# AFNO inverse on quarters of the TensorE array, and a remainder that is reordered through scratch

## The chip, the cores and the metric

The kernel runs on one core of one Trainium2 chip. The metric is the device time of one execution in microseconds: 1413.34 us before the change (median of 3 runs, 1412.42 to 1414.71). The engines are named as in the profile: PE (TensorE matmul), PEld (its weight loads), DVE (VectorE), ACT (ScalarE), POOL (GpSimd) and SP (SyncE, which only issues transfers here).

## The reference

One block on x of 4096 tokens with 640 channels. A condition vector c gives six modulation rows. First a spectral layer (AFNO): layer norm, modulation, a real FFT over the 4096 tokens, a two-layer complex MLP on each frequency in 4 blocks of 160 channels, a soft shrink, the inverse FFT. Then a SwiGLU feed-forward layer.

```python
Xf = rfft2(x, axes=(1, 2));  z = Xf.reshape(B, H, Wf, NB, BS);  zr, zi = z.real, z.imag
hr = relu(zr @ w1[0] - zi @ w1[1] + b1[0]);  hi = relu(zi @ w1[0] + zr @ w1[1] + b1[1])
or_ = hr @ w2[0] - hi @ w2[1] + b2[0];       oi_ = hi @ w2[0] + hr @ w2[1] + b2[1]
or_, oi_ = softshrink(or_, 0.01), softshrink(oi_, 0.01)
A = irfft2(or_ + 1j * oi_, s=(H, W), axes=(1, 2))

h = layernorm(x) * (1 + ca) + sa;   x = x + ga * A(h)
h = layernorm(x) * (1 + cb) + sb;   x = x + gb * ((silu(h @ w_gate) * (h @ w_up)) @ w_down)
```

## The kernel before

**Two parts.** The spectral part fills the first 310 us or so of the profiled execution, the feed-forward part the rest. The change is in the spectral part alone.

**The spectral part.** The transform over 4096 = 128 x 32 tokens is done in two factors. The first (`dft_a`) writes its result to scratch in DRAM (`s1`). The frequencies are then worked through in 8 chunks of 4 blocks, 32 places `p` in all, with chunk `ch = p // 4` and block `b = p % 4`. Chunk 4 (`CE`) has two more columns, for the frequencies that the others don't hold.

For a chunk, `load_g` fetches its part of `s1` and `stage_b` applies the second factor: five products `pb` per chunk, `t` = 0 to 3 for the first 128 channels of each block, and `t` = 4 for the **remainder**, the last 32 channels of all four blocks together on 128 partitions. `stage_l1` is the first MLP layer of a block, `stage_l2` the second, whose sums go to `tt`.

**fp32 from split parts.** The two layers need fp32 accuracy from fast fp32r products. An operand is split into a high part (the value rounded to fp32r by an ACT copy) and a low part (the difference, by DVE), and high x high, low x high and high x low are summed. `evac_b` makes both parts `z` of one `pb`. The remainder is different: `stage_l1` wants, for each block, the high parts of its 32 real and 32 imaginary rows and the low parts of both, one below the other, as one operand `rz` of 128 rows. `evac_rh` (ACT, line 630) and `evac_rl` (DVE, line 640) copy it 32 rows at a time, two ACT and two DVE instructions per block.

**The inverse.** After the last block of a chunk, `move_x` moves `tt` into four tiles `xx` (by DMA within SBUF, 64 real rows above 64 imaginary rows), `shrink_parts` (ACT) and `shrink` (DVE) do the soft shrink, `shrink_high` (ACT, line 752) and `shrink_low` (DVE, line 757) split `xx` into `xh` and `xl`. `stage_i` then applies the inverse of the second factor with the constant matrix `bm`, itself in a high and a low part: three fp32r products of 128 rows by 128 columns on each half of the 640 channels (lines 768 to 770), two ACT copies into `co`, and a store of `co` to scratch `s2` by POOL's queue. The matrix has two independent blocks of 64 x 64, for the two values of the index `p` in `constants()`; the rest of it is zero. Chunk 7, the last, has its inverse done in another way (`inverse_last`, line 825: fp32 products on 64 rows with the matrix `bx`).

**What sets the order.** The order of this part is written out by hand, place by place, in one loop over `p`; each engine executes its own instructions in that order and waits by semaphores. In a place stand the L1 layer of block `p`, the `stage_b` of a later block, the L2 layer of block `p - 1` and the inverse of `p - 7`. All transfers named here, but the stores of `co`, are issued by SP, in program order: a DMA that waits holds up those behind it. The first places also see SP finish the stores of `s1` (line 355), which precede `idn`, `tx` and `bx`. `fst`, `first_mm` and the lines from 947 on prepare the feed-forward part; they need the last `s2` rows (`load_first_rows`, line 832).

Memory places: SBUF pools hold tiles by tag with a number of buffers; a tag that changes size would shift its neighbours.

Of the kernel before, what the change touches and what calls it, by code (L numbers as in the profile page):

```python
# [6 lines left out]
F32 = mybir.dt.float32  # L7
# [39 lines left out]
def constants():  # L47
# [65 lines left out]
    bm = bm.reshape(2, 128, 128)  # L113
    bi = bm[1].reshape(2, 64, 128)

    bx = np.tile(bm[1].reshape(2, 64, 128).transpose(1, 0, 2), (2, 1, 1)).reshape(128, 256)
# [57 lines left out]
def body(tc, x, w1, b1, w2, b2, wg, wu, wd, c, wm, k_fa, k_tb, k_tx, k_bm, k_bx, k_ga, k_ge, k_id, out, dbg=None):  # L174
# [27 lines left out]
    with ExitStack() as top:  # L202
# [35 lines left out]
        with ExitStack() as af:  # L238
# [4 lines left out]
            bm = wp.tile([P, 2, 2, 128], F32R, name="bm")  # L243
# [345 lines left out]
            hss = {}  # L589

# [12 lines left out]
            def evac_b(ch, t):  # L603
                pb = pbs[ch, t]
                z = lp.tile([P, 2, 2, 258], F32R, tag="z", bufs=4, name=f"z{ch}_{t}")
                zs[ch, t] = z
                act.activation(z[:, 0, :, 0:256], pb, AF.Identity, scale=ca1[:, t:t + 1])
                dve.scalar_tensor_tensor(z[:, 1, :, 0:256], pb, ca1[:, t:t + 1],
                                         f32(z[:, 0, :, 0:256]), op0=OP.mult, op1=OP.subtract)
# [12 lines left out]
            def evac_rh(ch, b):  # L622
                pb = pbs[ch, 4]
                if b == 0:
                    rzs[ch] = hp.tile([P, NB, 258], F32R, tag="rz", bufs=2, name=f"rz{ch}")
                    if ch == CE:
                        pool.tensor_copy(rzs[ch][:, :, 257], zero.rearrange("p a b c d -> p (a b c d)")[:, 0:4])
                q = slice(32 * b, 32 * b + 32)
                for i in range(2):
                    act.activation(rzs[ch][32 * i:32 * i + 32, b, 0:256], pb[q, i, :], AF.Identity,  # L630
                                   scale=ca1[q, 4:5])

            def evac_rl(ch, b):
                pb = pbs[ch, 4]
                r = rzs[ch]
                q = slice(32 * b, 32 * b + 32)
                for i in range(2):
                    rh = slice(32 * i, 32 * i + 32)
                    rl = slice(64 + 32 * i, 96 + 32 * i)
                    dve.scalar_tensor_tensor(r[rl, b, 0:256], pb[q, i, :], ca1[q, 4:5],  # L640
                                             f32(r[rh, b, 0:256]), op0=OP.mult, op1=OP.subtract)
                    if ch == CE:
                        pool.tensor_copy(r[rh, b, 0:257:256], f32(edge[q, 0, 4, i]))
                        pool.tensor_copy(r[rl, b, 0:257:256], f32(edge[q, 1, 4, i]))
# [82 lines left out]
            def move_x(ch, i):  # L727
                q, h = i // 2, i % 2
                xx = p2.tile([P, D], F32, tag="xx", bufs=5, name=f"xx{ch}_{i}")
                for r in range(2):  # L730
                    nc.sync.dma_start(xx[64 * r:64 * r + 64, :], tts[ch, q][64 * h:64 * h + 64, r, :])
                xxs[ch, i] = xx
# [15 lines left out]
            def shrink_high(ch, i):  # L748
                xx = xxs[ch, i]
                xh = p2.tile([P, D], F32R, tag="xh", bufs=2, name=f"xh{ch}_{i}")  # L750
                xl = p2.tile([P, D], F32R, tag="xl", bufs=2, name=f"xl{ch}_{i}")
                act.activation(xh, xx, AF.Copy)
                xxs[ch, i] = (xh, xl, xx)

            def shrink_low(ch, i):
                xh, xl, xx = xxs[ch, i]
                dve.tensor_tensor(xl, xx, f32(xh), op=OP.subtract)

            def stage_i(ch, i):
                J = 4 * ORDER[ch] + i  # L760
                kd = 0 if J == 0 else 1
                xh, xl, _ = xxs[ch, i]
                co = p2.tile([P, D], F32, tag="xh" if 4 * ch + i == LAST - 1 else "co", bufs=2, name=f"co{J}")
                for hf in range(2):
                    e = slice(320 * hf, 320 * hf + 320)
                    pi = (bank0(0, [P, 512], f"pi{J}_{hf}") if ch == NCH - 2 and i % 2 and hf == 0 else
                          ps.tile([P, 512], F32, tag="p3", name=f"pi{J}_{hf}"))
                    mm(pi[:, :320], bm[:, kd, 0, :], xh[:, e], start=True, stop=False)
                    mm(pi[:, :320], bm[:, kd, 0, :], xl[:, e], start=False, stop=False)
                    mm(pi[:, :320], bm[:, kd, 1, :], xh[:, e], start=False, stop=True)  # L770
                    act.activation(co[:, e], pi[:, :320], AF.Copy)  # L771
                pool.dma_start(s2[4 * J:4 * J + 4].rearrange("k n d -> (k n) d"), co)  # L772
# [64 lines left out]
            for p in range(LAST + 1):  # L837
# [19 lines left out]
                rows = [p + 2] * (p < 4) + [p + 3] * (p > 2)  # L857
# [4 lines left out]
                for f in (shrink_high, tail_l1) if p == LAST else (tail_l1, shrink_high):  # L862
                    on(f, p if f == tail_l1 else p - 6)
# [4 lines left out]
                if p == LAST:  # L868
                    on(shrink_low, p - 6)
# [11 lines left out]
                on(stage_i, p - 7)  # L881
                if p < LAST:
                    on(shrink_low, p - 6)
                    on(shrink_parts, p - 5)
                if b == 0 and ch:
                    for i in range(4):
                        move_x(ch - 1, i)
                if p == 0:
# [3 lines left out]
                    pool.dma_start(bm.rearrange("p a b c -> p (a b c)"), k_bm)  # L892
# [11 lines left out]

            def load_first():
# [5 lines left out]
            for f in (shrink, shrink_high, shrink_low):  # L911
                on(f, LAST - 5)
            on(stage_i, LAST - 6)
            for p in range(LAST + 1, NP):
# [3 lines left out]
                if p == NP - 1:  # L918
                    on(shrink_high, p - 5)
                on(tail_l1, p)  # L920
                if p == NP - 1:
                    on(shrink_low, p - 5)
# [14 lines left out]
                if p < NP - 1:  # L937
                    on(shrink_high, p - 5)
                on(stage_l2, p - 1)
                on(stage_i, p - 6)  # L940
                if p < NP - 1:
                    on(shrink_low, p - 5)
            on(shrink, LAST - 1)
            on(shrink_high, LAST - 1)
# [4 lines left out]
            on(shrink_low, LAST - 1)  # L949
# [62 lines left out]
            for i in range(3):  # L1012
                xns[0].append(p2.tile([P, D], F32, tag="co" if i < 2 else "wm", bufs=2 if i < 2 else 1, name=f"xn0_{i}"))
# [1525 lines left out]
```

## Time and profile before

| | us |
|---|---|
| timed runs | 1412.42, 1413.34, 1414.71 |
| profiled execution, first to last instruction (the page gives no other time for it) | 1409.5 |
| median of the timed runs less that span | 3.8 |
| PE busy in it | 1382.5 (98%) |
| the loop from 109 to 257 us: PE, ACT, DVE busy of 148.0 | 147.95, 140.88, 131.67 |
| the 56 halves of the inverse: ACT copies of the result (line 771) | 22.6 |
| clock of PE over the span | 1.00 |

Rows of a timeline give the start, the time from the first start to the last end, engine, line, operation, output<-inputs, shape and count; matmuls are pipelined, so that a row's length is longer than what it adds. Rows of groups give the busy time, the mean ns of one, and the idle time before them with what ended it. Rows of transfers give the count, the size of each and the median time from issue to landing. In product shapes, 64*128 is 64 rows of the array by 128 columns. `SPq` is SP's queue of issues.

### The profile page before, as it was taken

How to read it: one execution, taken by the hardware profiler on the slowest of the kernel's cores; microseconds unless marked ns; L12 is line 12 of the kernel's file. 1: busy time of each engine (PE TensorE's matmuls, PEld its weight loads, DVE VectorE, ACT ScalarE, POOL GpSimd, SP SyncE). 2: the span in 40 equal slices, each digit the busy share in tenths (PEclk: the TensorE clock that was granted, in tenths of full speed). 3: DMA queues.
4: the chain of work that ended last, by engine and by line, in shares of the span. 5: the costliest groups of instructions: out<-in, count | busy, mean ns of one | idle time of the engine just before them, and what ended most of it. 6: DMA issues, size and time to landing. Idle time of an engine off the chain costs nothing. (4 is left out here: it accounts for less than half of the span.)

```text
span 1409.5 us, 23754 instructions
## 1 busy us (share of the span) xinstructions
PE 1382.5 (98%) x8410; PEld 1310.7 (93%) x8410; DVE 1067.8 (76%) x1861; ACT 765.0 (54%) x1542; POOL 604.6 (43%) x683
## 2 busy tenths in 40 slices
PE   6899999999999999999999999999999999999998
PEld 2599999967999889899999999999999999999998
DVE  8889888889888888649787668678678757375644
ACT  6879999755555554436454345546164624262341
POOL 5700200157766594326445534447153624042241
PEclk9999999999999999999999999999999999999999
DMA  9876466675998897898877998696998668956634
GB/s 371 310 244 211 157 196 193 203 232 170 327 353 308 308 335 263 293 368 308 308 225 281 375 330 288 236 326 230 375 330 309 217 218 282 350 194 217 199 115 149
DMA packets 171016, 377.34 MB, mean 268 GB/s; under 512 B 22193, under 2 KB 81649, under 8 KB 168882
## 3 DMA queue, kind: packets, MB, share of 16 engines
q1 hardware_dynamic: 161794, 359.28, 73.6%
q0 software_dynamic: 6800, 13.93, 3.1%
q10 hardware_dynamic: 2304, 2.62, 0.5%
q8 instruction: 66, 1.08, 0.3%
q14 instruction: 52, 0.43, 0.1%
HBM read 269.48 MB, written 96.80 MB: 260 GB/s over the span
## 5 line engine op out<-in xcount | busy, mean ns | idle before, releaser
L1442 DVE TENSOR_TENSOR wb<-r,wb 128x768 fp32r<-128x768 f32 (+3 forms) x170 | 170.4, 1013 | 13.5 <-ACT wb L1435 13.3
L2050 PE MATMUL pw<-h,wt 128*128 128x384 f32 x412 | 139.3, 338 | 0.6 <-ACT s_y L2069 0.6
L2052 PE MATMUL pw<-h,wt 128*128 128x384 f32 x412 | 138.3, 336 | 0.0
L2051 PE MATMUL pw<-h,wt 128*128 128x384 f32 x412 | 138.1, 335 | 0.0
L1435 ACT ACTIVATE wb<-r 128x768 fp32r<-128x768 f32 (+3 forms) x168 | 104.5, 639 | 56.3 <-PE pw L2063 41.7
L2351 PE MATMUL pc<-wq,L 128*128 128x320 f32 x846 | 132.7, 309 | 0.9 <-DMA wq<-wqd 0.9
L2110 POOL TENSOR_TENSOR sg<-s_x,sg 128x384 f32<-128x384 f32 x24 | 30.0, 1250 | 234.5 <-DVE s_x L2076 234.5
L2351 PEld LDWEIGHTS pc<-wq,L 128*128 128x128 f32 x846 | 126.3, 188 | 1.1 <-DVE x L2308 1.1
L2130 DVE TENSOR_TENSOR L<-sg,L 128x384 fp32r<-128x384 f32 x144 | 101.0, 725 | 27.7 <-ACT L L2126 27.2
L2069 ACT ACTIVATE s_x<-pw 128x384 f32<-128x384 f32 x52 | 25.6, 492 | 164.2 <-PE pw L2052 162.3
L2050 PE MATMUL pw<-h,wb 128*128 128x384 f32 x312 | 105.0, 336 | 0.0
L2051 PE MATMUL pw<-h,wb 128*128 128x384 f32 x312 | 104.4, 335 | 0.0
L2052 PE MATMUL pw<-h,wb 128*128 128x384 f32 x312 | 104.4, 335 | 0.0
L2121 POOL TENSOR_TENSOR sg<-sg,sg 128x384 f32<-128x384 f32 x72 | 91.9, 1276 | 23.4 <-DVE L L2130 20.0
L1973 PE MATMUL pg<-ht,wb 128*128 128x512 f32 x260 | 101.8, 392 | 0.0
L2351 PE MATMUL pe<-wq,L 128*128 128x320 f32 x648 | 101.7, 309 | 0.0
L1974 PE MATMUL pg<-ht,wb 128*128 128x512 f32 x260 | 101.3, 390 | 0.0
L1975 PE MATMUL pg<-ht,wb 128*128 128x512 f32 x260 | 101.2, 389 | 0.0
L2267 PE MATMUL pd<-wq,a 128*128 128x320 f32 x632 | 96.8, 310 | 0.0
L2351 PEld LDWEIGHTS pe<-wq,L 128*128 128x128 f32 x648 | 96.6, 188 | 0.0
L2267 PEld LDWEIGHTS pd<-wq,a 128*128 128x128 f32 x632 | 93.5, 188 | 0.5
L772 POOL DMA_DIRECT2D s<-co x28 | 15.7, 559 | 175.9 <-ACT co L771 175.9
(317 smaller groups left out, 3914.1 us busy)
## 6 DMA issues: line engine op xcount, KB each, us to landing
wq<-wqd SPq DMA_DIRECT2D x83, 640.0 KB, 6.1
wt<-td SPq DMA_DIRECT2D x103, 512.0 KB, 5.4
hs<-ho SPq DMA_DIRECT2D x52, 512.0 KB, 5.2
h<-hs SPq DMA_DIRECT2D x32, 768.0 KB, 7.9
td<-wt SPq DMA_DIRECT2D x25, 512.0 KB, 6.3
r<-in_B_w_gate_dram SPq DMA_DIRECT2D x24, 384.0 KB, 4.4
r<-in_B_w_up_dram SPq DMA_DIRECT2D x24, 384.0 KB, 4.3
xx<-tt SPq DMA_DIRECT2D x56, 160.0 KB, 3.3
```

The source lines that it names most:

```text
L1435: def high(ks, e=slice(0, c), copy=lambda o, i: act.activation(o, i, AF.Copy)):
L1442: dve.tensor_tensor(wbs[t, n][:, 1, ks, e], raw[t, n][:, ks, e], f32(wbs[t, n][:, 0, ks, e]), op=OP.subtract)
L1973: mm(b, wh, hh, start=(kk == 0), stop=False)
L1974: mm(b, wh, hl, start=False, stop=False)
L1975: mm(b, wl, hh, start=False, stop=(kk == 4))
L2050: mm(b, w(0, kp), a[:, kp, 0], start=start and kp == 0, stop=False, skip_group_check=not start)
L2051: mm(b, w(0, kp), a[:, kp, 1], start=False, stop=False, skip_group_check=not start)
L2052: mm(b, w(1, kp), a[:, kp, 0], start=False, stop=kp == 1, skip_group_check=not start)
L2121: pool.tensor_tensor(o, x, y, op=op)
L2130: dve.tensor_tensor(o[:, 1], raws[j], f32(o[:, 0]), op=OP.subtract)
L2267: mm(b[:, :320], l, m, start=start and i == 0, stop=stop and i == len(s) - 1)
L2351: mm(o[:, :320], ls[q][:, x, k], w[:, q, y], start=start and q == 0 and n == 0, stop=q == 1 and n == 2, skip_group_check=not start)
```

## The change

**Inverse.** `bm` becomes one fp32 matrix without parts: for each of the two blocks (`u`) on its 64 rows, the two variants `kd` of 64 columns. `xx` keeps real and imaginary rows interleaved as they stand in `tt`, so one DMA of 64 x 2 rows replaces two. `shrink_high` and `shrink_low` are gone. `stage_i` makes four fp32 products of 64 rows by 64 columns: block `u` takes rows `64u`, channel half `e` goes to the output rows `64e`, so that each of the four uses another quarter of the array; the two `u` write two PSUM banks, `e` the two halves of their partitions. The store is two DMAs of 64 partitions, with runs of 320 elements in place of 640. `stage_i` comes one place earlier (`p - 6`).

**Remainder.** Chunk 0 keeps its copies of 32 rows. For chunks 1 to 7 the remainder is evacuated by one `evac_b` like the other four, into a tile `zr`, and `move_r` writes its four parts (high real, high imaginary, low real, low imaginary; 128 partitions x 1 KB each) to scratch `rzd` and reads them back as `rz` in the wanted order: four DMAs out, one in, all on SP at the end of the place in which it is evacuated.

**Places.** `bm` is loaded by SP in place of POOL. The freed tags are balanced by a third buffer for `co` and a tile `spare`, so that other tiles stay where they are.

PE in the loop, the end of one place and the inverse in it (here the first place of chunk 3; `pc` is the L2 layer, `pi` the inverse, `pl` the L1 layer of the next place). Before:

```order
L711 MATMUL pc_0_1_1521<-w2a,h_0_0_1352 128x320 x3
L711 MATMUL pc_0_1_1521<-w2b,h_0_1_1366 128x320 x3
L711 MATMUL pc_0_1_1521<-w2c,r_2_0_1378 128x320 x2
L768 MATMUL pi_0_1532<-xh_2_1392,bm 128x320
L769 MATMUL pi_0_1532<-xl_2_1393,bm 128x320
L770 MATMUL pi_0_1532<-xh_2_1392,bm 128x320
L768 MATMUL pi_1_1537<-xh_2_1392,bm 128x320
L769 MATMUL pi_1_1537<-xl_2_1393,bm 128x320
L770 MATMUL pi_1_1537<-xh_2_1392,bm 128x320
L661 MATMUL pl_2_0_1551<-z_2_1287,w1a 128x256 x3
```

The same place with the change:

```order
L717 MATMUL pc_0_1_1489<-w2a,h_0_0_1338 128x320 x3
L717 MATMUL pc_0_1_1489<-w2b,h_0_1_1352 128x320 x3
L717 MATMUL pc_0_1_1489<-w2c,r_2_0_1364 128x320 x2
L763 MATMUL pi_0_1500<-xx_3_1060,bm 64x320
L763 MATMUL pi_1_1501<-xx_3_1060,bm 64x320
L763 MATMUL pi_0_1500<-xx_3_1060,bm 64x320
L763 MATMUL pi_1_1501<-xx_3_1060,bm 64x320
L667 MATMUL pl_2_0_1523<-z_2_1282,w1a 128x256 x3
```

Six products became four, between the same neighbours, and the tile is that of the next block (`xx_3`, not the parts of `xx_2`).

SP from the last store of `s1` to the first moves of `xx` (places 0 to 4). Before:

```order
L355 DMA s<-xa_122 64x4x640
L508 DMA idn<-in_k_id_dram 128x128
L509 DMA tx<-in_k_tx_dram 128x2
L531 DMA bx<-in_k_bx_dram 128x256
L308 DMA g_898<-s 128x1x2560
L298 DMA tb_900<-in_k_tb_dram 128x512
L536 DMA wm_0_987<-in_w_mod_dram 128x640
L731 DMA xx_0_1062<-tt_0_797 64x640 x2
```

With the change:

```order
L353 DMA s<-xa_122 64x4x640
L506 DMA idn<-in_k_id_dram 128x128
L507 DMA tx<-in_k_tx_dram 128x2
L529 DMA bx<-in_k_bx_dram 128x256
L886 DMA bm<-in_k_bm_dram 128x128
L623 DMA rzd<-z_4_863 4x32x256 x4
L625 DMA rz_900<-rzd 128x4x256
L306 DMA g_902<-s 128x1x2560
L296 DMA tb_904<-in_k_tb_dram 128x512
L534 DMA wm_0_983<-in_w_mod_dram 128x640
L736 DMA xx_0_1054<-tt_0_797 128x1x640
```

`bm`, the four stores of chunk 1's remainder and the load behind them now stand between `bx` and the load of `g` for chunk 2.

```diff
-    bm = bm.reshape(2, 128, 128)
     bi = bm[1].reshape(2, 64, 128)
-    bmh, bml = _hl(bm)
-    bm = np.stack([bmh, bml], axis=1)
-    bm = np.ascontiguousarray(bm.transpose(2, 0, 1, 3)).reshape(128, 2 * 2 * 128)
+    bm = np.stack([bm[:, :, u, :, u].reshape(2, 64, 64) for u in range(2)])
+    bm = bm.reshape(2, 2, 2, 32, 64).transpose(0, 3, 2, 1, 4).reshape(128, 128)
...
+            rzd = [nc.dram_tensor(f"rzd{i}", (4, 32, NB, 258), F32, kind="Internal").ap() for i in range(2)]
...
-                z = lp.tile([P, 2, 2, 258], F32R, tag="z", bufs=4, name=f"z{ch}_{t}")
+                z = (lp.tile([P, 2, 2, 258], F32R, tag="z", bufs=4, name=f"z{ch}_{t}") if t < 4 else
+                     hp.tile([P, 2, 2, 258], F32R, tag="zr", bufs=1, name=f"z{ch}_{t}"))
...
+            def new_r(ch):
+                rzs[ch] = hp.tile([P, NB, 258], F32R, tag="rz", bufs=2, name=f"rz{ch}")
+
+            def move_r(ch):
+                NN = width(ch)
+                d = rzd[ch % 2]
+                for q in range(4):
+                    nc.sync.dma_start(d[q, :, :, :NN].rearrange("r b e -> b r e"), f32(zs[ch, 4][:, q // 2, q % 2, :NN]))
+                new_r(ch)
+                nc.sync.dma_start(f32(rzs[ch][:, :, :NN]), d[:, :, :, :NN].rearrange("q r b e -> (q r) b e"))
...
-                for r in range(2):
-                    nc.sync.dma_start(xx[64 * r:64 * r + 64, :], tts[ch, q][64 * h:64 * h + 64, r, :])
+                nc.sync.dma_start(xx, tts[ch, q][64 * h:64 * h + 64])
...
             def stage_i(ch, i):
                 J = 4 * ORDER[ch] + i
                 kd = 0 if J == 0 else 1
-                xh, xl, _ = xxs[ch, i]
-                co = p2.tile([P, D], F32, tag="xh" if 4 * ch + i == LAST - 1 else "co", bufs=2, name=f"co{J}")
-                for hf in range(2):
-                    e = slice(320 * hf, 320 * hf + 320)
-                    pi = (bank0(0, [P, 512], f"pi{J}_{hf}") if ch == NCH - 2 and i % 2 and hf == 0 else
-                          ps.tile([P, 512], F32, tag="p3", name=f"pi{J}_{hf}"))
-                    mm(pi[:, :320], bm[:, kd, 0, :], xh[:, e], start=True, stop=False)
-                    mm(pi[:, :320], bm[:, kd, 0, :], xl[:, e], start=False, stop=False)
-                    mm(pi[:, :320], bm[:, kd, 1, :], xh[:, e], start=False, stop=True)
-                    act.activation(co[:, e], pi[:, :320], AF.Copy)
-                pool.dma_start(s2[4 * J:4 * J + 4].rearrange("k n d -> (k n) d"), co)
+                xx = xxs[ch, i]
+                co = p2.tile([P, 2, 320], F32, tag="co", bufs=3, name=f"co{J}")
+                pi = [bank0(0, [P, 512], f"pi{J}_0") if ch == NCH - 2 and i % 2 and u == 0 else
+                      ps.tile([P, 512], F32, tag="p3", name=f"pi{J}_{u}") for u in range(2)]
+                for e in range(2):
+                    for u in range(2):
+                        k = slice(64 * u, 64 * u + 64)
+                        mm(pi[u][64 * e:64 * e + 64, :320], bm[k, kd], xx[k, 320 * e:320 * e + 320], start=True, stop=True)
+                for u in range(2):
+                    act.activation(co[:, u], pi[u][:, :320], AF.Copy)
+                for e in range(2):
+                    pool.dma_start(s2[4 * J:4 * J + 4, :, 320 * e:320 * e + 320].rearrange("(u k) n d -> (k n) u d", u=2),
+                                   co[64 * e:64 * e + 64])
...
                 for q in todo:
                     stage_b(*q)
-                    if q[1] < 4:
+                    if q[1] < 4 or q[0]:
                         evac_b(*q)
...
-                rows = [p + 2] * (p < 4) + [p + 3] * (p > 2)
+                rows = [p + 2] * (p < 2)
...
-                on(stage_i, p - 7)
+                on(stage_i, p - 6)
...
+                if todo and todo[0][1] == 4:
+                    move_r(todo[0][0])
...
-                    pool.dma_start(bm.rearrange("p a b c -> p (a b c)"), k_bm)
+                    nc.sync.dma_start(bm.rearrange("p a b -> p (a b)"), k_bm)
...
+            p2.tile([P, 3 * D], F32, name="spare")
```

`shrink_high` and `shrink_low` and all calls of them are removed.

More of the change, by code (lines that the diff above doesn't have):

```diff
@@ L242, in body @@
             w1c = qp.tile([P, NB, 640], F32R, tag="wq", name="w1c")
-            bm = wp.tile([P, 2, 2, 128], F32R, name="bm")
+            bm = wp.tile([P, 2, 2, 128], F32, name="bm")[:, 0, 0].rearrange("p (a b) -> p a b", a=2)
             tx = wp.tile([P, 2], F32, name="tx")
@@ L624, in evac_rh @@
                 if b == 0:
[L625 to L627 removed]
+                    new_r(ch)
                 q = slice(32 * b, 32 * b + 32)
@@ L746, in shrink @@
                     dve.tensor_tensor(xx, xx, cl, op=OP.subtract)
[L748 to L757, printed above, removed]
             def stage_i(ch, i):
@@ L861, in body @@
                     weights_high(*prep2[4])
-                for f in (shrink_high, tail_l1) if p == LAST else (tail_l1, shrink_high):
-                    on(f, p if f == tail_l1 else p - 6)
+                on(tail_l1, p)
                 if p == 0:
@@ L908, in load_first @@
                 x2s[0] = x2
-            for f in (shrink, shrink_high, shrink_low):
-                on(f, LAST - 5)
-            on(stage_i, LAST - 6)
+            on(shrink, LAST - 5)
             for p in range(LAST + 1, NP):
```

20 lines of the change are left out of this document (2 added, 18 removed).

## The prediction

> **What bounds the kernel now.** I read the table of stretches first, since a mean over the whole span mixes stages; then the order of events of one step; then groups, transfers and the last steps of the spectral part.
>
> ```profile
> PE 1382.5 (98%) x8410; PEld 1310.7 (93%) x8410; DVE 1067.8 (76%) x1861; ACT 765.0 (54%) x1542; POOL 604.6 (43%) x683
> 109.00:257.00 148.00, 147.95 (x1159) 147.06 (x1158) 131.67 (x253) 140.88 (x289) 17.51 (x52) 1.00 0.60 193
> ```
>
> The second row (length, then busy time of PE, weight loads, DVE, ACT, POOL, then clock and DMA share) covers most of the loop that the change edits. PE is busy for 147.95 of 148.00 us. ACT is close behind (140.88), DVE too (131.67), but neither makes PE wait: work taken off them is worth nothing there. What counts is the time of the inverse on PE, and any wait that is new.
>
> ```profile
> 152.42 0.31 PE L768 MATMUL pi<-xh,bm 128*128 128x320 f32 x1
> 152.57 0.31 PE L769 MATMUL pi<-xl,bm 128*128 128x320 f32 x1
> ...
> 153.16 0.31 PE L770 MATMUL pi<-xh,bm 128*128 128x320 f32 x1
> 153.30 0.52 PE L661 MATMUL pl<-z,w1a 128*128 128x256 f32 x3
> ...
> 159.04 0.30 PE L768 MATMUL pi<-xh,bm 128*128 128x320 f32 x1
> ```
>
> One inverse occupies PE from 152.42 to 153.30, 0.88 us, six products 0.15 apart. A whole step of the loop is 159.04 - 152.42 = 6.6 us.
>
> **The change part by part. 1: split parts and remainder copies go.**
>
> ```profile
> L752 ACT ACTIVATE xh<-xx 128x640 fp32r<-128x640 f32 x28 | 20.3, 726 | 6.7 <-DVE xx L746 6.5
> L757 DVE TENSOR_TENSOR xl<-xx,xh 128x640 fp32r<-128x640 f32 x28 | 22.8, 814 | 0.9 <-ACT xh L752 0.8
> L630 ACT ACTIVATE rz<-pb,ca 32x256 fp32r<-32x256 f32 x64 | 29.8, 466 | 1.6 <-DVE rz L640 0.5 <-PE pb L600 0.2
> L640 DVE SCALAR_TENSOR_TENSOR rz<-pb,ca,rz 32x256 fp32r<-32x256 f32 x64 | 30.9, 483 | 7.1 <-ACT rz L630 5.9
> L607 ACT ACTIVATE z<-pb,ca 128x512 fp32r<-128x512 f32 x32 | 22.1, 689 | 6.4 <-PE pb L600 5.7
> L608 DVE SCALAR_TENSOR_TENSOR z<-pb,ca,z 128x512 fp32r<-128x512 f32 x32 | 24.0, 749 | 10.2 <-ACT z L607 10.1
> ```
>
> ACT loses 28 x 0.73 and 56 x 0.47 (8 of the 64 stay, for chunk 0) and gains 7 x 0.69: 42 us less. DVE loses 28 x 0.81 and 56 x 0.48 and gains 7 x 0.75: 45 us less. On the path this is nothing as long as PE is full; if PE had been waiting for them, up to the few waits of part 4 would be gained.
>
> **2: the inverse on quarters.** Four fp32 products of 64 rows by 64 columns take the place of six full ones. No quarter runs in this trace; the nearest rows are products on half the rows (64*128), which sit alternately in the upper and the lower half.
>
> ```profile
> 284.81 1.35 PE L825 MATMUL pi<-tt,bx 64*128 64x320 f32 x8 [0.53 <-ACT co L771]
> 287.51 1.34 PE L825 MATMUL pi<-tt,bx 64*128 64x320 f32 x4
> 300.44 2.32 PE L983 MATMUL py<-tt,et 128*128 128x320 f32 x8
> L825 PE MATMUL pi<-tt,bx x32: 429/429/533, 284.8 to 305.3; 64*128 64x320 f32 x32
> 302.60 0.70 PE L988 MATMUL py<-cfrr,et 112*128 112x320 f32 x2
> 303.23 0.53 PE L825 MATMUL pi<-tt,bx 64*128 64x320 f32 x1
> 286.10 0.41 PE L768 MATMUL pi<-xh,bm 128*128 128x320 f32 x1
> 286.35 0.31 PE L769 MATMUL pi<-xl,bm 128*128 128x320 f32 x1
> L711 PEld LDWEIGHTS pc<-w2a,h 128*128 128x128 f32 x192 | 29.8, 189 | 0.4
> L711 PEld LDWEIGHTS pc<-w2a,h 128*2 128x2 f32 x12 | 1.0, 83 | 0.2
> 179.70 0.45 PE L711 MATMUL pc<-w2c,r 128*128 128x320 f32 x2
> 179.99 0.38 PE L711 MATMUL pc<-w2a,h 128*2 128x160 f32 x3
> ```
>
> An fp32 product appears as two passes. Eight passes of full width take 2.32 us, the last of them 0.43 from start to end, so passes follow each other every (2.32 - 0.43)/7 = 0.27. The first row holds both halves, eight passes in 1.35; the second row one half alone, four passes in 1.34. So two row halves run side by side, the second 0.01 behind. Four quarters side by side would stream for 2 x 0.27 + 3 x 0.01 = 0.57.
>
> Coming in and going out costs something. In front: the two L988 passes start at 302.60 and 302.87 and have streamed by 303.14; the half-array's load starts at 303.23, 0.09 later. Behind: the eight passes of the first row end at 286.16, so the last began at 285.73 and had streamed by 286.00; the next product starts at 286.10, 0.10 later, and its successor 0.25 after it in place of 0.15, another 0.10, because its weights could not be loaded ahead. A load of 128 columns takes 189 ns and one of 2 columns 83, so 64 columns exposed on the way in cost some 0.05. Together 0.09 + 0.05 + 0.57 + 0.10 + 0.10 = 0.91, against 0.88: **+0.03, times 28 = +0.8 us**.
>
> Bounds: below, no cost of coming in or going out, 0.57, which is -0.31 x 28 = -8.7 us. Above, four products one after another: 8 x 0.27 + 0.34 = 2.50, +45 us; that is excluded in part, as row halves do overlap: two at a time is 4 x 0.27 + 0.34 + 0.01 = 1.43, +15 us. I take 0.91, because the half-array rows are the nearest.
>
> The last two rows speak for the lower bound: between the full products and those of two columns (128*2, placed in a strip of 32 columns) there is no gap: 179.70, 179.85, 179.99. The Trainium skill, TensorEngine Tiling (Array Packing), Key Properties, says that a change of the tiling mode drains the engine. The half-array rows agree (0.09 and 0.10), these last rows do not. By the rule the sum stays +0.8, by the last rows it is -8.7.
>
> The inverse comes one place earlier (two places after its transfer). Its shrink is done at the beginning of that place, about 5 us ahead, so nothing new waits. Its store becomes two DMAs on POOL, which is idle for 130 of 148 us. The eight xx moves per chunk become four of twice the size: free.
>
> **3: the remainder through scratch.** For chunks 2 to 7 it is evacuated three steps (20 us) ahead of its first use, and the four stores and the load need about 8 us: hidden. Chunk 1 is different.
>
> ```profile
> 66.30 11.38 SPq L355 DMA_DIRECT2D s<-xa  x10
> 77.72 1.37 SPq L508 DMA_DIRECT2D idn<-in_k_id_dram  x1
> ...
> 80.42 0.95 SPq L531 DMA_DIRECT2D bx<-in_k_bx_dram  x1
> 81.61 0.57 SPq L308 DMA_DIRECT2D g<-s  x1
> ...
> 84.76 0.59 PE L661 MATMUL pl<-z,w1a 128*128 128x256 f32 x3
> 85.55 0.40 PE L661 MATMUL pl<-rz,w1c 128*128 128x256 f32 x2
> 92.30 5.02 SPq L731 DMA_DIRECT2D xx<-tt  x8
> s<-cz ACTq DMA_DIRECT2D x4, 160.0 KB, 2.5
> wm<-in_w_mod_dram SPq DMA_DIRECT2D x20, 320.0 KB, 3.1
> g<-s SPq DMA_DIRECT2D x5, 320.0 KB, 3.9
> g<-s SPq DMA_DIRECT2D x6, 1280.0 KB, 7.2
> ```
>
> SP is late: it still issues the stores of s1 until 77.7 and is at bx until 81.4. The data are ready by then; the queue is what is late. Behind bx now stand bm, four stores of 128 KB and, once these have landed, the load of 512 KB. At SP's pace (5.02/8 = 0.63) bm takes until 82.0 and the fourth store is issued at 82.0 + 3 x 0.63 = 83.9. It lands 2.5 later as s<-cz does, at 86.4, and the load 3.1 to 3.9 after that, at 89.5 to 90.3. PE wants rz at 85.55. So **PE waits 4.0 to 4.8 us in the first place of chunk 1, where it waits for nothing now; I take +4.2**. Bounds: both transfers as fast as 2.5, +3.3; the store as slow as under load (the 7.2 of a 1280 KB g load) and the load at 3.9, 83.9 + 11.1 - 85.55 = +9.5. Behind the blocked SP stand g and tb of chunk 2: g now goes at about 87 in place of 81.61, lands by 87 + 7.2 = 94.2, and is wanted a step or more after 85.55 plus the wait (85.55 + 6.6 + 4.2 = 96.4): in time, by 2 us. Nothing behind gives the wait back, since PE is full from there to 257.
>
> **4: the last steps.**
>
> ```profile
> 261.76 0.31 PE L770 MATMUL pi<-xh,bm 128*128 128x320 f32 x1
> 262.16 0.41 PE L768 MATMUL pi<-xh,bm 128*128 128x320 f32 x1
> 283.36 0.74 ACT L752 ACTIVATE xh<-xx 128x640 fp32r<-128x640 f32 x1 [2.18 <-DVE xx L746]
> PEld py L988 <- DMA cfrr<-s: 0.4, 1, 0.4
> ```
>
> Here PE does wait: 0.40 in place of 0.15 at 262.16, and 0.53 at 284.81, where a bank is freed by an ACT copy that stands behind the 0.74 of xh. Both go with xh and xl: -0.8, and some -0.2 of similar size between. More than that is capped by the last store and its reload, for which PE waits at L988. **-1.0**, bounds 0 and -2.
>
> Sum: +0.8 + 4.2 - 1.0 = +4.0 on the profiled execution's span of 1409.5, so 1413.5. The median is 3.8 above that span; I carry this unchanged: 1413.34 + 4.0 = **1417.3 us**.
>
> **The rivals.** *A: quarters on the same rows queue.* Only row halves are seen to overlap. If the second column half of a row half starts once the first is in its second pass, three passes are in a row: 3 x 0.27 + 0.37 = 1.18, +0.30 x 28 = +8.4, so 1413.3 + 8.4 + 3.2 = 1425. The Trainium skill, TensorE: Matmul & The Clock Gate, Part 3, has the rule that a weight load overlaps running products only when the row group differs, which gives this case; the 1.35 us row agrees for different rows, and no row shows the same rows. *B: column halves do not overlap at all:* 1.43, +15.4, so 1432. *C: faster.* The quarters come and go without a gap, as the 128*2 products do: -8.7 + 4.2 - 1.0 = -5.5, so 1408. It decides once a quarter inverse takes less than 0.88 - 3.2/28 = 0.77. Against it: all three half-array edges shown have their gap. *D: the wait at chunk 1 is covered,* because DMA is quicker than any row here: +0.8 - 1.0, so 1413.
>
> **How the numbers follow.** Forecast 0.44, A 0.22, B 0.08, C 0.20, D 0.06. A run of this kernel tells about 0.2% (2.8 us) from no change: faster is below 1410.5, slower above 1416.2. C is faster in 0.16 and the same in 0.04; the forecast is slower in 0.32 and the same in 0.12 (a wait of 3.3 with -1.0 or more at the end); D is the same; A and B are slower. Faster 0.16, same 0.22, slower 0.62. The range takes in C's and A's times: 1407 to 1430; the forecast's own is 1414 to 1421.
>
> **What would show it.** Right: a first product of quarters and the product behind the last one some 0.9 apart, 28 times; a PE wait of about 4 us for a DMA into rz in the first place of chunk 1, and none in later chunks; ACT and DVE some 40 us less busy; the rest of the program shifted by 4 us. Wrong: quarters 1.2 or 1.4 apart (A, B) or below 0.77 (C), no PE wait for rz (D), or a wait for rz in any later chunk.

## The result, and the profile after

The changed kernel takes 1430.86 us (median of 1424.83, 1428.48, 1433.23 and 1434.23) against 1412.95 us for the kernel before (median of four executions): a ratio of 1.0125, 95% interval 1.0095 to 1.0155. It is slower by 17.9 us. The forecast was 1417.3 us, slower by 4; the time lies just past the end of its range (1430).

The profiled execution is the fastest of the four (1424.83 us, span 1423.0). Its engines, on the page:

```profile
PE 1384.5 (97%) x8466; PEld 1295.4 (91%) x8466; DVE 1025.1 (72%) x1784; ACT 722.7 (51%) x1465; POOL 620.0 (44%) x696
```

Five stretches of it, with length, then busy time of PE, weight loads, DVE, ACT and POOL, then the granted clock, the DMA share and GB/s:

```profile
109.00:257.00 148.00, 147.31 (x1189) 132.75 (x1188) 101.93 (x195) 107.97 (x231) 27.46 (x57) 1.00 0.73 220
82.00:92.00 10.00, 0.69 (x6) 0.48 (x5) 2.06 (x4) 0.69 (x1) 0.00 (x0) 0.74 0.39 124
92.00:97.00 5.00, 4.70 (x22) 4.70 (x23) 1.33 (x3) 2.06 (x5) 0.00 (x0) 0.50 0.87 327
97.00:100.00 3.00, 3.00 (x23) 3.00 (x23) 1.78 (x4) 0.99 (x2) 0.00 (x0) 0.99 0.04 11
268.00:271.00 3.00, 2.95 (x14) 2.95 (x15) 1.96 (x3) 1.25 (x4) 0.00 (x0) 0.50 1.04 365
```

ACT and DVE have 42 us less to do each, and in the loop (109 to 257) PE is as full as before. But from 82 to 92 us PE stands nearly still, and then it works at half clock until 97. The same comes again, shorter, at 264 to 271. The timeline of the first place of chunk 1, in which `rz` is first read from scratch:

```profile
79.81 2.31 SPq L623 DMA_DIRECT2D rzd<-z  x4
81.74 0.59 PE L667 MATMUL pl<-z,w1a 128*128 128x256 f32 x3
88.34 0.58 SPq L625 DMA_DIRECT2D rz<-rzd  x1
92.30 0.80 PE L667 MATMUL pl<-rz,w1c 128*128 128x256 f32 x2 [9.62 <-DMA rz<-rzd]
99.57 0.52 PE L667 MATMUL pl<-z,w1a 128*128 128x256 f32 x3
```

The last of the four stores is issued at 81.6, and until 88.2, 6.6 us later, SP waits for them to land; then it issues the load. PE waits 9.62 us. The place takes 99.57 - 81.74 = 17.83 us; before it took 5.90. What the DMA engines do meanwhile, in 40 slices from 82 to 88 us (tenths busy of all 16; then the one queue's packets, MB and share):

```profile
DMA  2222312232222222222313222222222222222000
q1 hardware_dynamic: 478, 0.47, 25.0%
```

The transfers fill a quarter of the 16 engines for 5.5 us, while nothing else is in flight. A store of `move_r` writes the shape 4 x 32 x 256 from 128 partitions. The Trainium skill (DMA: Bandwidth & Descriptors, Why a DMA increments its semaphore by 16 and not by 1) says that a transfer runs on the largest number of engines, up to 16, that divides the count of the slowest dimension on both of its sides; for 4 and 128 that is 4. The 25.0% agrees.

Chunk 7 waits too, in the first place where its remainder is used:

```profile
247.71 1.91 SPq L534 DMA_DIRECT2D wm<-in_w_mod_dram  x1
249.93 0.69 SPq L828 DMA_DIRECT2D cfrm<-s  x1
250.66 0.59 SPq L828 DMA_DIRECT2D cfrr<-s  x1
251.36 2.81 SPq L623 DMA_DIRECT2D rzd<-z  x4
263.96 0.59 SPq L625 DMA_DIRECT2D rz<-rzd  x1
268.05 0.79 PE L667 MATMUL pl<-rz,w1c 128*128 128x256 f32 x2 [2.72 <-DMA rz<-rzd]
```

Here SP issues the stores 7.8 us into the place (it starts at 243.59), behind moves of `xx`, a load of `wm` and the first load of finished rows (`load_first_rows`, 2 x 320 KB); the last of them is issued by 254.2, and they have landed 9.8 us later.

The end of the spectral part, where PE waits for the last `s2` rows, and the first gate product of the feed-forward part (`pg`):

```profile
302.08 1.18 POOL L767 DMA_DIRECT2D s<-co  x2 [4.30 <-ACT co L765]
307.03 0.33 SPq L828 DMA_DIRECT2D cfrm<-s  x1
309.90 1.31 PE L972 MATMUL py<-cfrm,et 112*128 112x320 f32 x4 [1.16 <-DMA cfrm<-s]
324.08 0.50 PE L1907 MATMUL pg<-ht,wb 128*128 128x512 f32 x1
```

The same product on the finished rows before, without a wait:

```profile
295.52 1.31 PE L988 MATMUL py<-cfrm,et 112*128 112x320 f32 x4
```

The inverse on quarters, between the second layer and the next first layer:

```profile
111.67 0.46 PE L717 MATMUL pc<-w2c,r 128*128 128x320 f32 x2
112.05 0.77 PE L763 MATMUL pi<-xx,bm 64*64 64x320 f32 x8
112.75 0.62 PE L667 MATMUL pl<-z,w1a 128*128 128x256 f32 x3
```

Eight passes, two for each of four quarters, from start to end in 0.77 us: they run side by side.

The balance by places, from the starts of each place's first product in the timelines of all kernels (us; the experiments follow below). Place 5, which has no column, takes 6.64 or 6.65 us in all of them. "Spread" means stores with 128 rows outermost, "late rows" the first load of finished rows behind chunk 7's `move_r`, "pairs" two inverses behind each other in every second place:

| profiled execution | 4 to 5 (chunk 1) | 6 to 28 | 28 to 29 (chunk 7) | 29 to first gate product | place 4 to first gate product |
|---|---|---|---|---|---|
| before | 5.90 | 156.57 | 9.34 | 46.53 | 224.99 |
| changed | 17.83 | 158.14 | 12.10 | 47.62 | 242.34 |
| quarters alone | 5.90 | 157.72 | 7.71 | 47.51 | 225.48 |
| scratch alone | 15.24 | 159.78 | 13.43 | 45.60 | 240.70 |
| changed, stores spread | 10.21 | 157.20 | 7.71 | 47.52 | 229.29 |
| stores spread, chunk 1's on POOL | 14.33 | 157.20 | 7.71 | 47.48 | 233.37 |
| the same, its loads on SP | 7.96 | 157.20 | 7.71 | 47.48 | 227.00 |
| chunk 1 by copies | 5.89 | 159.00 | 15.40 | 47.51 | 234.45 |
| chunk 1 by copies, late rows | 5.90 | 158.37 | 7.76 | 47.49 | 226.17 |
| chunk 1 by copies, spread | 5.91 | 157.20 | 7.71 | 47.30 | 224.77 |
| the same, late rows | 5.90 | 157.20 | 7.71 | 47.59 | 225.05 |
| chunk 1 by copies, spread, pairs | 5.90 | 152.98 | 10.04 | 47.32 | 222.89 |
| the same, late rows | 5.91 | 152.97 | 8.16 | 47.57 | 221.26 |
| the same, last pair | 5.90 | 152.99 | 8.16 | 45.55 | 219.25 |

From place 4 to the first gate product the change costs 242.34 - 224.99 = 17.35 us, which is nearly the difference of the medians; the span differs by 13.5 only, because this execution was 3.0 us quicker up to place 4 (starts of place 0 lie between 56.35 and 60.06 us in the profiles of all kernels) and 0.8 us quicker in the feed-forward part.

### The profile page after: what moved, and what is told of

Read it like the earlier page. It is cut to its first block, busy times and chain, and to the rows that moved or that the text cites. A ratio compares the mean times of both kernels' runs of the same rounds, so it can differ in the third digit from the quotient of the medians.

```text
span 1423.0 us, 23711 instructions
## 1 busy us (share of the span) xinstructions
PE 1384.5 (97%) x8466; PEld 1295.4 (91%) x8466; DVE 1025.1 (72%) x1784; ACT 722.7 (51%) x1465; POOL 620.0 (44%) x696
## 5 line engine op out<-in xcount | busy, mean ns | idle before, releaser
L767 POOL DMA_DIRECT2D s<-co x56 | 33.4, 601 | 180.8 <-ACT co L765 180.1
```

## The experiments

The theory T put to the test: the loss is made by the way through scratch, by two waits for `rz` and the half clock after each; the quarters cost next to nothing. Its rival R1: the quarters cost it. Times stand beside the kernel before on the same chip (1412.4 to 1413.3 us).

**Each half of the change alone.**

Quarters alone, from the changed kernel: the remainder of every chunk by `evac_rh` and `evac_rl` again, no `move_r` (`COPY` lists the chunks that are copied).

```diff
+            COPY = (0, 1, 2, 3, 4, 5, 6, 7)
...
-                    if q[1] < 4 or q[0]:
+                    if q[1] < 4 or q[0] not in COPY:
...
-                rows = [p + 2] * (p < 2)
+                rows = [k for k in [p + 2] * (p < 4) + [p + 3] * (p > 2) if k // 4 in COPY]
...
-                if todo and todo[0][1] == 4:
+                if todo and todo[0][1] == 4 and todo[0][0] not in COPY:
                     move_r(todo[0][0])
```

Scratch alone, from the kernel before: `zr`, `rzd` and `move_r` as in the change, the inverse untouched.

```diff
-                    if q[1] < 4:
+                    if q[1] < 4 or q[0]:
                         evac_b(*q)
...
+                if todo and todo[0][1] == 4:
+                    move_r(todo[0][0])
```

> The inverse on quarters as in the changed kernel, the remainder of every chunk by copies as before. Theory T (the loss is made by the way through scratch: two waits of TensorE for rz, 9.9 us in chunk 1 and 3.0 us in chunk 7, TensorE at half clock after each, 2.4 and 1.7 us, and a later end): about 0.5 us for 28 quarter inverses at 0.02 us and the px gap, so 1411 to 1415 us, a clock of 1.0 throughout and no wait for rz. Rival R1 (the quarters cost it, by switching or by what they do to the clock): 1424 us or more.

> The remainder of chunks 1 to 7 through scratch as in the changed kernel, the inverse before it (xh, xl, three products per half, one store). T: nearly the whole loss, 1425 to 1433 us, with a wait for rz of 9 to 10 us at the first place of chunk 1, a half clock for about 10 us around it, and a second wait in chunk 7. R1: within 3 us of the kernel before.

Quarters alone: 1412.43 us, ratio 1.000 (0.998 to 1.002). Scratch alone: 1429.02 us, 1.012 (1.008 to 1.016). R1 falls; the loss is on the side of scratch (from place 4 to the first gate product the quarters alone cost 225.48 - 224.99 = 0.49 us). In scratch alone another wait shows, 2.0 us for the edge columns of chunk 4, put down to the DMA that loads its `g`, which stands behind `move_r` on SP.

**The shape of the stores.**

```diff
-            rzd = [nc.dram_tensor(f"rzd{i}", (4, 32, NB, 258), F32, kind="Internal").ap() for i in range(2)]
+            rzd = [nc.dram_tensor(f"rzd{i}", (4, P, 258), F32, kind="Internal").ap() for i in range(2)]
...
-                    nc.sync.dma_start(d[q, :, :, :NN].rearrange("r b e -> b r e"), f32(zs[ch, 4][:, q // 2, q % 2, :NN]))
+                    nc.sync.dma_start(d[q, :, :NN], f32(zs[ch, 4][:, q // 2, q % 2, :NN]))
                 new_r(ch)
-                nc.sync.dma_start(f32(rzs[ch][:, :, :NN]), d[:, :, :, :NN].rearrange("q r b e -> (q r) b e"))
+                for q in range(4):
+                    nc.sync.dma_start(f32(rzs[ch][32 * q:32 * q + 32, :, :NN]), d[q, :, :NN].rearrange("(b r) e -> r b e", b=NB))
```

> The changed kernel with scratch laid out so that each store is 128 rows of 1 KB, outermost count 128 in place of 4; the load is four loads of 32x4x256. T with the cause 'stores on four of the sixteen DMA engines': the stores of chunk 1 land within 2.5 to 3.5 us of the last issue (6 us before), the wait for rz falls from 9.9 us to 5 to 7, the one in chunk 7 goes; 1419 to 1424 us. Rival R3 (the stores are slow because writing to scratch is, or because of other traffic, whatever their shape): stores still land 6 us and 10 us late, 1427 to 1434 us.

1418.16 us, ratio 1.0033 (1.0017 to 1.0048): 12.7 us of the 17.9 are gone. In the view of transfers from 70 to 100 us (KB of each, median us from issue to landing) and the timeline:

```profile
rzd<-z SPq DMA_DIRECT2D x4, 128.0 KB, 3.3
rz<-rzd SPq DMA_DIRECT2D x4, 128.0 KB, 2.5
```

```profile
88.59 0.47 PE L668 MATMUL pl<-rz,w1c 128*128 128x256 f32 x2 [2.59 <-DMA rz<-rzd]
```

The wait falls from 9.62 to 2.59 us, below the 5 to 7 expected: a load of one part waits for its own store alone, and the first went out at 84.38, 3.3 us after the first store. Chunk 7 does not wait any more (7.71), nor does chunk 4's edge. The stores land in 3.3 us in place of 6.6, to the same scratch and from the same queue, and the 6.6 were reached with nothing else in flight, so R3 falls. The edit changes two things, the shape of the stores and the one load that became four; how much of the shorter wait each is worth was not separated.

**The late SP.** With the stores spread, chunk 1's were issued on POOL, which is idle there (`eng`), once with its loads too, once with the loads left on SP.

```diff
+                eng = pool if ch == 1 else nc.sync
...
-                    nc.sync.dma_start(d[q, :, :NN], f32(zs[ch, 4][:, q // 2, q % 2, :NN]))
+                    eng.dma_start(d[q, :, :NN], f32(zs[ch, 4][:, q // 2, q % 2, :NN]))
```

> As the kernel with spread stores, and chunk 1's four stores and four loads issued on GpSimd, which stands idle there, in place of SyncE, where they stood behind scratch stores and four loads of constants until 79.8 us. T: stores issued from about 76.5 us, rz there by about 84 us: wait of 0 to 2 us, no half clock, no wait in chunk 7; 1412 to 1418 us. If the late SyncE is not part of it: as the kernel with spread stores alone.

> The kernel with the spread stores of chunk 1 on GpSimd, its four loads back on SyncE, ahead of the load of g for chunk 2 (1.28 MB). With all eight on GpSimd the loads took 6.8 us to land in place of 2.5 us, beside that load of g, and the wait was 5.8 us. Theory C (it was the collision with g, which SyncE's order had kept behind the loads): loads land in 2.5 to 3 us again, the wait falls to 1 to 3 us, 1415 to 1419 us. Rival (GpSimd's own queue is slow, stores 5.8 us against 3.3, and that sets it): wait of 4 to 6 us, 1420 to 1423 us.

The first gave 1421.55 us (1.0068, 1.0047 to 1.0089), 3.4 us more than with everything on SP, against the expectation of 1412 to 1418. The stores went out earlier, but SP, with nothing of chunk 1 left to wait for, now sent the load of `g` of chunk 2 (1.28 MB) in front of the loads of `rz`. Its timeline, and its view of transfers:

```profile
77.57 2.28 POOL L624 DMA_DIRECT2D rzd<-z  x4 [9.95 <-ACT z L607]
80.47 0.62 SPq L306 DMA_DIRECT2D g<-s  x1
92.95 0.77 PE L669 MATMUL pl<-rz,w1c 128*128 128x256 f32 x2 [5.83 <-DMA rz<-rzd]
```

```profile
rz<-rzd POOLq DMA_DIRECT2D x4, 128.0 KB, 6.8
```

The loads were issued from 84.0 to 86.5. From 84 to 87 us the DMA queues (packets, MB, share of the 16 engines; `q1` is SP's here, `q0` POOL's) show:

```profile
q1 hardware_dynamic: 144, 0.94, 91.5%
q0 software_dynamic: 1, 0.00, 0.0%
```

From 87 to 88 us the shares are 94.6% and 5.0%, from 88 to 89 they are 42.1% and 64.0%: the loads moved only as SP's transfers thinned out.

The second: 1416.39 us (1.0030, 1.0015 to 1.0044). The same two views:

```profile
87.33 0.47 PE L669 MATMUL pl<-rz,w1c 128*128 128x256 f32 x2 [1.92 <-DMA rz<-rzd]
```

```profile
rz<-rzd SPq DMA_DIRECT2D x4, 128.0 KB, 2.7
```

The loads land in 2.7 us again. Together with the rows of the queues this speaks for the collision with `g` and what was sent behind it; but the run also took the loads off POOL's queue, so that this queue is slow with loads by itself is not excluded. The late SP was worth 0.7 us of wait only (2.59 to 1.92): the stores from POOL took 6.7 us, beside the transfers of `s1` and of the constants, with which the DMA engines move 382 to 398 GB/s from 75 to 81 us. As the half clock went with it, the place is 10.21 - 7.96 = 2.25 us shorter in the profile; the two ratios, 1.0033 and 1.0030, do not tell the kernels apart.

**Chunk 1 by copies, as chunk 0.** `move_r` from chunk 2 on, the rows of chunk 1 copied at places 2 to 4; with the stores as changed, then spread.

> The changed kernel with chunk 1 by copies like chunk 0; chunks 2 to 7 through scratch with the stores as changed (outermost count 4). T, chunk 1 being 9.9 us of wait and about 2.4 us of half clock behind it: 12 to 14 us below the changed kernel, 1416 to 1420 us; no wait for rz before chunk 7, where 2 to 4 us and a half clock of 3.4 us remain. If chunk 1's wait were paid anyway by something else that is late there (the loads of g and tb for chunk 2): over 1424 us.

> The same with the spread stores: neither chunk 1 nor chunk 7 waits. T: what is left is the quarters (about 0.5 us) and the later end (about 1 us): 1412 to 1416 us, clock 1.0 after the start, although ScalarE and VectorE have about 35 us less to do than before. If the freed engines are worth anything: under 1411 us.

1422.36 us (1.0077, 1.0050 to 1.0105), more than the 1416 to 1420 expected, and 1415.28 us (1.0023, 1.0006 to 1.0039), within its range. Chunk 1's wait is gone, but chunk 7's grows from 2.72 to 4.99 us: its stores land 1.7 us later in the place than in the changed kernel, and no row says why. With spread stores no wait for `rz` is left in the profile.

**Chunk 7: shape or order.** The first load of finished rows goes behind `move_r` of chunk 7.

```diff
-                if p == LAST - 4:
+                if p == LAST - 3:
                     cf += [rp.tile([P, 2, D], F32, tag=tag, name=f"cf{tag}") for tag in ("rm", "rr")]
                     load_first_rows(rb + 16, rl, nc.sync)
```

> The kernel with chunks 0 and 1 by copies, the stores as changed (outermost count 4), the load of finished rows behind chunk 7's move. With the load ahead the step from place 28 to 29 took 15.4 us, with spread stores 7.7 us. S: the stores are issued 3 us earlier and land in about 6 us rather than 10: the step falls to 7.7 to 9 us. If the shape of the stores alone made the wait in chunk 7: still over 12 us.

One run, 1413.46 us; the step is 7.76 us instead of 15.40, with the stores still on four engines. The timeline, in which PE's first product with `rz` has no wait:

```profile
242.67 3.02 SPq L624 DMA_DIRECT2D rzd<-z  x4
254.23 0.57 SPq L626 DMA_DIRECT2D rz<-rzd  x1
258.11 0.44 PE L673 MATMUL pl<-rz,w1c 128*128 128x256 f32 x2
```

They land 8.5 us after the last issue has ended, not in 6, but that is just enough: the load lands as PE comes to the product. In these profiles either remedy, the shape or the order, removes chunk 7's wait.

> The kernel with chunks 0 and 1 by copies and spread stores, with the load of finished rows behind chunk 7's move, one inverse in each place. It stands to the one with pairs and late rows as one change to the array's quarters stands to two. T on the change: 4.2 us between places 6 and 28 are the pairs' and show in the time too: 1414 to 1416.5 us, against 1411.96 us with pairs. On the 2.9 us by which scratch for chunks 2 to 7 stood over copies, with no wait in the profiled runs: if they are a wait of chunk 7 in some of the runs, they go here, 1412 to 1413.5 us; if they are half clocks after waits in the feed-forward part (a 3.4 us period at 320 to 330 us in one profile, at 500 to 510 us in another), they stay.

Both together: 1412.97 us, 1.0005 (0.9991 to 1.0019). That is below the 1414 to 1416.5 that would show the pairs' saving, and within the 1412 to 1413.5 expected for a wait of chunk 7 in some of the executions, but the profiles with and without late rows show the same step (7.71), and the intervals of 1.0023 and 1.0005 overlap: that such a wait went is not shown.

**Pairs.** If the change into the quarters and back has a price of its own, two inverses behind each other should save one. Scratch frees the bank of the remainder (`bank0(1)`) after one evacuation, where the copies hold it over several places, so the second of a pair finds room. The kernel is the one with chunk 1 by copies and spread stores; the argument 1 gives an inverse the two `bank0` banks.

```diff
-                on(stage_i, p - 6)
+                if p % 2 == 0:
+                    on(stage_i, p - 7, 1)
+                    on(stage_i, p - 6)
```

> The kernel with chunks 0 and 1 by copies and spread stores, and two inverses behind each other in every second place up to the first of chunk 7 (11 pairs, eight quarter products in a row, the second inverse in the banks of B, which scratch has made free), in place of one in each. A quarter inverse costs 0.9 us, of which its four products by two side by side are 0.57 us; the other 0.34 us lie at the change into the quarters and back. T: one change in two is saved, 11 x 0.34 = 3.7 us: 1408 to 1412 us, 2.5 to 4.5 us below the kernel with one inverse in each place. If the cost is by product and not by change: no difference.

> The kernel with pairs of inverses, and the first load of finished rows (cfrm and cfrr, 1.3 MB) behind chunk 7's move instead of ahead of it on SyncE. With pairs the step from place 28 to 29 took 10.04 us, 7.71 us without a wait. Theory S (chunk 7's stores stood behind that load on SyncE, 235.0 to 238.2 us, and its traffic made them land 4.7 us late): the step falls to 7.7 us, the span by 2.3 us, 1409 to 1412 us. Rival (the stores are late whatever stands ahead of them): still over 9.5 us.

Pairs: 1413.04 us (0.999, 0.997 to 1.001), above the 1408 to 1412 expected, and 2.2 us below the kernel without pairs. From place 6 to 28 they take 157.20 - 152.98 = 4.22 us less, but not all of that is saved: the inverse of place 27 now stands in place 28. The pairs also shorten the three places that chunk 7's stores and load have, by 1.1 us, and its wait came back, with 1.64 us (28 to 29: 10.04). With late rows, which are 640 KB and not the 1.3 MB of the expectation: 1411.96 us (0.9984, 0.9970 to 0.9998). The step 28 to 29 is 8.16 and not 7.71, without a wait, as it holds the second inverse of a pair. From place 6 to 29, against the same kernel without pairs: 157.20 + 7.71 - 152.97 - 8.16 = 3.78 us, 0.34 for each of 11 changes, just as expected. The time is 0.2% below that kernel (1.0005), but the two intervals overlap, so that the saving is shown by the profiles alone. A pair and what follows it, in the kernel of the next experiment:

```profile
143.99 1.31 PE L770 MATMUL pi<-xx,bm 64*64 64x320 f32 x16
145.22 0.63 PE L674 MATMUL pl<-z,w1a 128*128 128x256 f32 x3
```

From first product to the first layer 1.23 us for two inverses, 0.70 us for one in the changed kernel.

**The end.**

```diff
             on(stage_i, LAST - 2)
+            on(stage_i, LAST - 1, 1)
...
             for i in range(2):
                 inverse_last(i, 0)
-            on(stage_i, LAST - 1)
```

> The same, with the last quarter inverse right behind the one before it, ahead of the last second-layer products, so that its two stores go out about 5 us earlier. T on the end (the wait of about 1 us for cfrm at the first feed-forward rows is for these two stores, which land 5.4 us after their issue where one store landed in 3.8): that wait goes, and one more change of the array is saved, about 0.4 us: 1 to 1.5 us below the kernel with late rows, 1407.5 to 1411 us. Rival (something else holds these rows, or TensorE waits for the clipped block instead): no gain.

1409.35 us, ratio 0.9969 (0.9954 to 0.9983): faster than both kernels, by 4.0 us than the one before. PE's first product with the finished rows `cf`, in the timeline of the kernel with pairs and late rows, where it waits:

```profile
293.61 1.31 PE L981 MATMUL py<-cfrm,et 112*128 112x320 f32 x4 [1.09 <-issue]
```

The same in this one, without a wait:

```profile
289.44 1.24 PE L981 MATMUL py<-cfrm,et 112*128 112x320 f32 x4
```

The stretch from place 29 to the first gate product falls by 47.57 - 45.55 = 2.02 us: the wait of 1.09; 0.70 from place 29 to the first block products (`py<-tt`, L976; 26.65 to 25.95), in which are a change of the array and, against it, a new wait of 0.51 us for `cz`; and some 0.2 us that no row names. In the kernel that waits, the profile names no releaser (`issue`); in the changed kernel it names the DMA of `cfrm`. That the wait goes when the stores are earlier speaks for the stores as its cause.

## Why the prediction was wrong

**Part 1, right.** ACT lost 42.3 us (42 predicted), DVE 42.7 (45). In the time it was worth nothing: with both parts of the change and no wait for `rz` left (chunk 1 by copies, spread, late rows), it is that of before (1.0005). In the profiles of that kernel and of the quarters alone, scratch in place of copies gains 157.72 - 157.20 = 0.52 us from place 6 to 28.

**Part 2, right.** The step of a place grew from 6.60 to 6.62 us where nothing else differs, against +0.03 predicted. The sum of 0.09 + 0.05 + 0.57 + 0.10 + 0.10 holds in its parts: 0.70 us from the first quarter to the next layer's product, next to 0.05 + 0.57 + 0.10 = 0.72, and a pair, which saves all but the 0.57, saves 0.34, as by the sum. So the quarters run side by side and the change of the array is not free: rivals A, B and C are out. So is D, as PE did wait for `rz`. That the measured 1430.86 us stands next to rival B's 1432 is chance.

**Part 3 failed, at three steps.** The mechanism named for chunk 1 was the right one, stores late on SP, their landing, the load, a wait of PE. The first wrong step is the term "it lands 2.5 later as s<-cz does": it measured 6.6 us from the issue of the last store (81.6 to 88.2). The row it was taken from was that of stores with 128 rows outermost; these have 4. The load took 4.0 us, next to the 3.1 to 3.9 predicted and 0.6 more than the 4.2 had reckoned with, and SP was 0.7 us later, against PE, than worked out (the last store at 81.6 in a place that starts at 81.74; worked out were 83.9 and 84.76). 4.2 + 4.1 + 0.6 + 0.7 make the 9.6 us of wait; the upper bound of 9.5 was reached for a reason it did not name.

The second wrong step is a missing term: what a long wait does to PE afterwards. The place lost 11.93 us, 9.62 of waiting and 2.3 more at a clock of 0.50.

The third is "for chunks 2 to 7 ... hidden", with 8 us for stores and load in 20 us. In chunk 7 SP came to the stores 7.8 us into the place, stores and load then took 251.36 to 268.05, 16.7 us, and the step 28 to 29 was 4.39 us longer than with the quarters alone, 2.72 of it waiting and the rest half clock. The place's own queue on SP had not been read: it holds the first load of finished rows. The prediction's last sentence had named a wait for `rz` in a later chunk as what would prove it wrong. Place 12, where chunk 4's edge columns are made, lost 0.95 us more (8.64 against 7.69), which the spread stores remove too.

**Part 4, half right.** In the step 28 to 29 the quarters alone gain 1.63 us, of which 0.80 is an inverse that moved to place 6. Of the other 0.83, 0.43 goes with the pause at 262.16 and the slower products behind it, and 0.3 with products that the part did not name (L558, which start 0.26 us sooner behind their neighbours and take 0.06 less). The other pause that it named, 0.53 at 284.81, is gone as well, but it lies behind place 29, and a new wait of 0.35 us for an ACT copy stands there: up to the first block products (`py<-tt`) the quarters alone gain 0.09 us (26.73 to 26.64). Then the reverse came: 47.51 us in place of 46.53 from place 29, because the last rows now go out in two stores and PE waits for them (0.98 us with the quarters alone); moving the last inverse ahead took that away. So -1.0 was about +0.15.

Sum against the span between place 4 and the first gate product: +11.93 in chunk 1, +1.57 up to place 28 (0.80 the moved inverse), +2.76 in 28 to 29, +1.09 at the end: +17.35, where +4.0 was predicted. What stays open: the three other executions of the changed kernel are 4 to 9 us longer than the profiled one, at mean clocks of 0.991 to 0.993 against 0.995; longer waits with longer half clocks would do it, but no row shows them. Part of it need not be the change's: the profiled one has the earliest start of place 0 of all profiles (56.35 us, the others up to 60.06), and the kernel before spreads as widely (1409.11 to 1419.62 us in 22 executions beside the first experiments).

## What to carry to other kernels

Take a DMA's duration only from a row of the same shape: here stores of 128 KB took 6.6 us to land with an outermost count of 4 and 3.3 us with 128, and the share of busy DMA engines showed it at once (25% with nothing else in flight). Where work goes from engines to a DMA queue, read that queue to the end at every place where the new transfers stand, not at the first alone, and add the clock's price to any wait of 2 us or more. An earlier issue on another queue can lose what it gains, if it lets a larger transfer of the old queue pass in front.

## What the runs showed of the hardware that was not expected

**Half clock after waits shorter than the slow stretch.** In the changed kernel with spread stores PE waited 2.59 us, ran for 1.0 us, and then had half the clock for 3.5 us. The table of stretches (clock behind POOL's busy time):

```profile
86.00:88.60 2.60, 0.01 (x1) 0.04 (x1) 2.06 (x4) 0.02 (x1) 0.00 (x0) 1.00 0.97 249
88.60:89.60 1.00, 1.00 (x8) 1.00 (x9) 0.00 (x0) 0.43 (x2) 0.00 (x0) 1.00 0.73 287
89.60:93.10 3.50, 3.50 (x19) 3.50 (x18) 1.33 (x3) 1.71 (x6) 0.00 (x0) 0.51 0.93 359
93.10:95.00 1.90, 1.90 (x15) 1.90 (x15) 1.20 (x3) 0.91 (x2) 0.00 (x0) 1.00 0.18 62
```

A wait of 2.72 us (chunk 7 of the changed kernel) did the same. So did one of 2.04 us with scratch alone, for chunk 4's edge columns, followed by ten products of two columns:

```profile
151.00:153.10 2.10, 0.06 (x2) 0.03 (x1) 1.63 (x3) 2.05 (x5) 0.00 (x0) 1.00 0.94 367
155.00:158.40 3.40, 3.40 (x15) 3.40 (x14) 0.88 (x3) 0.00 (x0) 0.47 (x2) 0.50 0.17 37
```

After 1.92 us (stores on POOL, loads on SP) the clock stayed at 1.00, and so it did after 1.64 us (pairs). The same table for the 1.92 us:

```profile
86.00:89.00 3.00, 1.67 (x14) 1.70 (x15) 1.75 (x5) 0.98 (x3) 0.00 (x0) 1.00 0.91 312
89.00:92.00 3.00, 3.00 (x25) 3.00 (x25) 2.05 (x5) 2.07 (x5) 0.00 (x0) 1.00 0.85 331
```

The Trainium skill (TensorE: Matmul & The Clock Gate, Part 1) gives half speed after an idle window of about 3.4 us. The length of the slow stretch agrees; the waits that brought it were shorter, and in the 3.6 us ahead of the slow stretch above PE ran for 1.0 us.

**Four fp32 quarters run side by side.** Two passes each, eight in 0.77 us from first start to last end. Four more behind them, the second inverse of a pair, add 1.23 - 0.70 = 0.53 us, where the six full fp32r products of an inverse before took 0.88. The change into the quarters and back costs 0.34 us (3.78 us for 11 changes).
